# A fused attention and mixer kernel: two additions from banks and the roots of two pairs moved to VectorE, and the loads of one pair begun a step sooner

## The chip, the core and the metric

The kernel runs on one core of one Trainium2 chip. Such a core has five engines, each with its own queue of instructions, which it works in order: TensorE (PE in the profile; its weight loads are PEld) multiplies matrices, VectorE (DVE) and ScalarE (ACT) work elementwise and on rows, GpSimd (POOL) does elementwise work too, and SyncE (SP) here only issues DMA transfers. TensorE writes to banks of PSUM; everything else lies in SBUF or in DRAM. Engines wait for each other by semaphores.

The metric is the device time of one execution in microseconds, start to end. A kernel's time is the median of several executions.

## The reference

Attention with normalized queries and keys, then one mixer layer, all in fp32:

```python
# B, H, S, D = 8, 12, 448, 64;  d_model = H*D = 768, d_tok = 256, d_ch = 1536
rmsnorm = lambda x, g: x / sqrt(mean(x * x, -1) + 1e-6) * g
scores = matmul(rmsnorm(q, g_q), rmsnorm(k, g_k).T) / sqrt(D)
attn = exp(scores - max(scores)); attn = attn / (sum(attn) + 1e-9)
x = concat_heads(matmul(attn, v))                     # (B, S, 768)
h = relu(x.T @ w_tok1) @ w_tok2                       # over the sequence
u = x + h.T
out = u + relu(u @ w_ch1) @ w_ch2                     # over the channels
```

The four mixer weights arrive in 64 bits and are converted on the chip. The eight batch entries are independent of each other but for the weights.

## The kernel before

**Pairs and elements.** The 96 heads are worked as 48 pairs of heads, six to a batch entry, which the text calls an element: pairs 0 to 5 belong to element zero, 6 to 11 to the next, 12 to 17 to element two, 18 to 23 to element three. The mixer of one element runs while the attention of the next one or two is computed between its products, so that TensorE always has work.

**Queries, keys and roots.** `Start.loads` (L1280) gives the DMAs of a pair: four for a *plain* pair (below 12), which lies in rows and is turned by TensorE, and eight of 56 KB for a pair from 12 on, which is loaded in *blocks* of 32 rows (L1296) and turned by VectorE's 32 x 32 transposes. A pair's q and k lie together in one of two slots (`qk_t[p % 2]`, L1287), so the loads of pair p + 2 wait until pair p has been turned. For each pair ScalarE squares (`square`, L1312, L1315), VectorE sums over the head dimension (`reduce`, L1329), and for pairs in blocks ScalarE copies the half sums across (`fold`, L1337). The inverse roots are made for two pairs at a time: a first guess from the bits of the number (`guess`, L1351, VectorE) and three Newton steps (`newton`, L1354). A step is four GpSimd instructions (L1359 to L1362) for pairs 2 to 11 and from pair 20 on (`far`, L1221), and otherwise three on VectorE (`newton_step`, L1370 to L1372). `scale` (L348, VectorE) multiplies the pair by the roots, and `turn_qk` (L350) transposes it.

**Attention steps.** Up to pair 17 the attention goes in small steps (`att_step(g)`, L584, with g = 4t + s and s from 0 to 3 for the two pairs 2t and 2t + 1): some of the scores (L386, with ScalarE's exponentials at L390), products with the values (L459), and beside them the preparation of the next two pairs. From t = 9 (`BIG`, L513) it goes in large blocks (`big_step`, L515), whose first one, in place of step 36, squares pairs 20 and 21 and takes their roots. In the kernel before, L691 loads pair 21 in step 35, and L682 loads pair 20 in the same step, eight DMAs each; steps 34 and 35 belong to pairs 16 and 17 and also turn pairs 18 and 19.

**Weights.** `weight_items` (L313) walks over the chunks of the raw weights: load (L181), four conversion instructions on VectorE (L273 to L278), one on ScalarE (L284), a last one on VectorE (L307), and a store (L197) of the converted chunk, called a *stage*, to DRAM. From a stage's four blocks GpSimd makes four sums (`make`, L209 to L212) for the products with fewer multiplications that the later elements use. For the first eight stages the blocks are loaded again into spare tiles called `few` (L226), added there and stored (L216); these rounds lie in the second half of element zero's products (`first_items`, L1059). The later elements read blocks and sums as *units* of 384 KB (`load_units`, L841), into eight tiles.

**The mixer.** Element zero uses the stages directly: `tok1` (L764), `tok2` (L806, whose bank VectorE adds to u at L811, one addition per 128 channels), then `first_stage` (L883) for each of the 36 stages, 18 of the channel mixer's first matrix and 18 of its second. Two banks of PSUM (`ps_M`, two buffers) take turns in all of these. A column of banks is closed six stages apart for the second matrix: stages 23, 29 and 35. There ScalarE copies each of two banks to SBUF (L903) and GpSimd adds it to u (L904). Two `turns` (L1015, VectorE) then transpose the last channels for the output, which goes out by 32 rows at a time.

Element one and the later ones have x turned through DRAM: VectorE transposes (L752), `send_x` (L714) writes to `xs`, `load_x` (L723, L726) reads it back. Then `tok1`, `tok2`, and `moving_sums` (L819), which makes four sums called T1 to T4 of u's quarters, the first two on VectorE, the last two on GpSimd. The products `ch1` (L922) and `ch2` (L979) run in the order of `PRODUCTS` (L817); the fourth of them reads T3. `ch2` adds to u by VectorE and GpSimd (L988).

**What sets the order.** On TensorE, VectorE, ScalarE and GpSimd the order is the program's own. The lists of work carry a cost with each item, and `merge` (L27) and `place` (L565) mix two lists in proportion to these costs; `later` (L119) puts a DMA off by some microseconds of the same costs. A changed list thus changes the places of what it is mixed with. SyncE's queue alone is ordered by the compiler's planner, by its own estimate of when each transfer is ready to go. SyncE then works it in order: a DMA that waits holds up all behind it.

Of the kernel before, what the change touches and what calls it, by code (L numbers as in the profile page):

```python
# [13 lines left out]
ALU = mybir.AluOpType  # L14
# [30 lines left out]
def whole(ctx, tc, shifted, pre, q, k, v, g_q, g_k, moe_w_tok1, moe_w_tok2, moe_w_ch1, moe_w_ch2, out):  # L45


    nc = tc.nc
# [64 lines left out]
    st = dict(pre.st)  # L113
# [317 lines left out]
    def on_pe(p):  # L431

        return shifted or p < NPAIR
# [14 lines left out]
    def values(ps, k):  # L448

        kw = dict(start=(k == 0), stop=(k == NK - 1))  # L450
        for p in ps:
            if k == 0:
                st["o", p] = ps_O.tile([P, 512], F32, name="o_ps")
                if on_pe(p):
                    st["d", p] = s_tile("d_ps") if shifted else m_tile()
            e, vt = exps(p, k), st["v", p]
            for a in range(2):
                rows = rows_of(p, a)
                nc.tensor.matmul(  # L459
                    out=st["o", p][a * D:(a + 1) * D, 0:S], lhsT=vt[rows, k * D:(k + 1) * D], rhs=e[rows, :], **kw)  # L460
        for p in ps:
            if on_pe(p):
                ones(p, exps(p, k), **kw)
        if not shifted:
            used(ps[0] // 2, k)
# [47 lines left out]
    BIG = NPAIR + NPAIR // 2  # L513
# [70 lines left out]
    def att_step(g):  # L584


        t, s = divmod(g, 4)
        p = 2 * t
        pair = (p, p + 1)
        live = g < NG  # L590
        items = []

        def finish():
            if s == 0 and t:
                last = (p - 2, p - 1)
                for k in (NK - 2, NK - 1):
                    values(last, k)
            if live:
                for k in ((0,), (1, 2), (3, 4), (5, 6))[s]:
                    score(t, k)  # L600
            if s == 0 and t:
                if not on_pe(p - 1):
                    row_sums(t - 1)
                for i in last:
                    st.pop(("v", i))

        def tiled():
            if shifted:
                if live:
                    both_shifted()  # L610
            else:
                finish()
            if live and s == 3:
                for i in pair:
                    st.pop(("qkT", i))
            if inside:
                for fn in turns:
                    fn()
            if live and s and not shifted:
                for k in ((), (0,), (1, 2), (3, 4))[s]:  # L620
                    values(pair, k)

        def both_shifted():
            i = p + s // 2
            if s % 2 == 0:
                score_shifted(i)
                return
            for k in range(NK):
                values((i,), k)
            for k in range((NK + 1) // 2):  # L630
                st.pop(("e1", i, k))
            st.pop(("v", i))
            for part in denominators((i,)):
                part()

        n = p + 2
        ahead, behind, turns = [], [], []
        f = lambda fn, *pairs: [lambda i=i: fn(i, st) for i in pairs]  # L640
        scales = lambda n: [lambda i=i: scale(i) for i in (n, n + 1)]
        if g in (1, 5):
            ahead, behind = f(pre.square, g // 4 * 2 + 4), f(pre.reduce, g // 4 * 2 + 4)
        elif g in (2, 6):
            ahead, behind = f(pre.square, g // 4 * 2 + 5), f(pre.reduce, g // 4 * 2 + 5)
        elif g in (3, 7):
            behind = pre.roots(g // 4 * 2 + 4, st)
        elif g in (4, 8):
            behind = scales(g // 4 * 2 + 2)
        if live and n < NP:  # L650
            late = n < 2 * NPAIR + 2
            if t >= NPAIR // 2 and late:
                if s == 1:
                    ahead, behind = f(pre.square, n), f(pre.reduce, n) + f(pre.square, n + 1)
                elif s == 2:
                    behind = f(pre.reduce, n + 1) + pre.roots(n, st) + scales(n)
            elif t >= NPAIR // 2:
                a, b = f(pre.square, n) + f(pre.reduce, n), f(pre.square, n + 1) + f(pre.reduce, n + 1)
                behind = (a, b + pre.roots(n, st), scales(n), [])[s]
            now = {2: [] if pre.plain(n) else [n], 3: [n, n + 1] if pre.plain(n) else [n + 1]}.get(s, [])  # L660
            turns = [lambda q=q, i=i: turn_qk(q, i) for q in now for i in (1, 0)]

        inside = g < 2 * NPAIR
        items += [(0.3, fn) for fn in ahead]
        items.append((2.4 if s == 1 else 3.2, tiled))
        part = lambda fns, c=0.4: [(c, fn) for fn in fns]
        if s == 0 and t and not shifted:
            items += part(denominators((p - 2, p - 1)))
        soon = s == 3 and not inside and not pre.plain(n)
        if soon:  # L670
            items += part(turns)
        if live and not on_pe(p):
            items += [(0.5, lambda k=k: group_sums(t, k)) for k in ((), (1, 2), (3, 4), (5, 6))[s]]

        if s == 0 and 5 < p + 1 < NP:
            items.append((0.0, lambda: load_v(p + 1)))
        if live and s == 1 and 5 < p + 2 < NP:
            items.append((0.0, lambda: load_v(p + 2)))
        js = []
        if live and s == 0:  # L680
            js = [n, n + 1] if pre.plain(p) else [n + 1]
        elif live and s == 3 and not pre.plain(n):  # L682
            js = [n + 2]
        items += [it for j in js if pre.first_slot + 2 <= j < NP
                  for it in part(pre.loads(j, st, nc.sync, nc.sync), 0.2 if pre.plain(j) else 0.6)]
        if g == 3:
            items += [it for j in (6, 7) for it in part(pre.loads(j, st, nc.sync, nc.sync), 0.2)]
        items += part(behind)
        if not inside and not soon:
            items += part(turns)  # L690
        if g == 4 * BIG - 1 and not shifted:  # L691
            items += part(pre.loads(n + 3, st, nc.sync, nc.sync), 0.3)
        return items


# [169 lines left out]
    def r_tile(i):  # L865
        return r_pool.tile([P, 2 * HS], F32, name=f"r{i}")
# [16 lines left out]
    def first_stage(n):  # L883

        w, _, m, t = stages[n]
        wide = w is moe_w_ch2
        last = (KF if wide else KC) - 1
        if t == 0:
            st["m", 0], st["m", 1] = m_tile(), m_tile()
        a, u = st.pop(("stage", n)), st["uT", 0]  # L890
        for o in range(2):
            ps = st["m", o][:, 0:S]
            for half in range(2):
                nc.tensor.matmul(  # L894
                    out=ps, lhsT=a[:, o + 2 * half, :],
                    rhs=natural(half)[:, :, t, :] if wide else u[:, half * KC + t, :],
                    start=(t == 0 and half == 0), stop=(t == last and half == 1))
            if t < last:
                continue
            if wide:  # L900

                to, c = u[:, o * KC + m, :], r_tile(1 + o)[:]
                nc.scalar.copy(out=c, in_=ps)  # L903
                nc.gpsimd.tensor_tensor(out=to, in0=to, in1=c, op=ALU.add)  # L904
            else:
                nc.scalar.activation(
                    out=natural(o)[:, :, m, :], in_=ps.rearrange("p (i n) -> p i n", i=2), func=AF.Relu)
        st["used"].add(("stage", n))
# [178 lines left out]
    stages = stage_list()  # L1087
# [20 lines left out]
    for p in (4, 5):  # L1108
# [7 lines left out]
        out=g_t[:, 0:1], in0=g_t[:, 0:1], scalar=float(D) ** 0.5, in1=g_t[:, 1:2],  # L1116
# [27 lines left out]
    for b in range(B):  # L1144
# [33 lines left out]
        elif b + AHEAD < B:  # L1178
            t = (b + AHEAD) * NPAIR // 2
# [18 lines left out]
class Start:  # L1198
# [155 lines left out]
    def newton(self, p, st, last):  # L1354
        nc, x, y = self.nc, st["x", p], st["y", p]
        t = self.nt_pool.tile([128, 56], F32, name="nt", tag="nt")[0:y.shape[0], 0:y.shape[1]]
        if 1 < p < 2 * self.NPAIR or p >= self.far:

            nc.gpsimd.tensor_tensor(out=t, in0=y, in1=y, op=ALU.mult)  # L1359
            nc.gpsimd.tensor_tensor(out=t, in0=t, in1=x, op=ALU.mult)  # L1360
            nc.gpsimd.tensor_scalar(t, t, -0.5, 1.5, ALU.mult, ALU.add)
            nc.gpsimd.tensor_tensor(out=y, in0=t, in1=y, op=ALU.mult)  # L1362
        else:
            self.newton_step(x, y, t)
        if last:
            del st["x", p], st["y", p]
# [80 lines left out]
```

## Time and profile before

The median of three executions was 1307.17 us, from 1307.05 to 1308.61. One more was profiled:

| quantity | value |
|---|---|
| profiled execution, whole | 1308.48 us |
| its span, first to last instruction | 1306.6 us |
| granted TensorE clock | 0.99 of full |
| TensorE busy | 1260.9 us (97%) |
| VectorE busy | 763.7 us (58%) |
| ScalarE busy | 375.9 us (29%) |
| GpSimd busy | 351.3 us (27%) |
| moved by DMA | 229.59 MB, 176 GB/s in the mean |

By stretches of the span the engines' busy time and the mean busy share of the 16 DMA engines are:

| stretch, us | what runs on TensorE | TensorE busy, us | VectorE, us | GpSimd, us | DMA share |
|---|---|---|---|---|---|
| 0 to 110 | attention of element zero | 90.59 | 89.11 | 22.52 | 0.75 |
| 110 to 284 | mixer of element zero, attention of element one | 162.05 | 123.59 | 47.23 | 0.74 |
| 284 to 435 | mixer of element one, attention of element two | 146.52 | 98.17 | 70.97 | 0.92 |
| 435 to 1306.6 | all that follows | 861.74 | 452.86 | 210.60 | 0.66 |

In the lines of the timeline that follow below, a line has the start in us from the span's start, the busy us, the engine, the kernel's line, the operation, the tiles written and read with partitions x elements, and how many instructions the line stands for; the bracket has the engine's idle time before it and what ended it. SPq is SyncE's queue of issues, and the us there are the time that the issues took. In lines of waits the numbers are the sum of the idle time in us, the count, and the longest. A tile's name stands for all its buffers: `m_ps` are the two banks of `ps_M`, `stage` the converted weights. Ends of matmuls are modelled, and times on GpSimd are rough.

### The profile page before, as it was taken

The numbers are of one execution on the slowest core, as the hardware profiler recorded it, in microseconds if no ns is written. First come the engines' busy times: TensorE is split into PE (matmuls) and PEld (weight loads), VectorE is DVE, ScalarE is ACT, GpSimd is POOL, SyncE is SP. The second block draws the span as 40 slices with busy tenths as digits, with TensorE's granted clock in tenths as the row PEclk, the third lists the DMA queues.
The fourth block names the chain that finished last, engine by engine and source line by source line (L and its number), as shares of the span: only waits on it lengthen the run. The fifth ranks groups of instructions, "written<-read, shape, count | busy, mean of one in ns | idle before, by whom it ended". The sixth has DMA issues, their size and how long they took to land.

```text
span 1306.6 us, 20357 instructions
## 1 busy us (share of the span) xinstructions
PE 1260.9 (97%) x7408; PEld 927.2 (71%) x7408; DVE 763.7 (58%) x1205; ACT 375.9 (29%) x752; POOL 351.3 (27%) x575
## 2 busy tenths in 40 slices
PE   5998999989998999999999999999999999999996
PEld 3444444447787687796778777896788868797996
DVE  6998868827774466645676366754656366433212
ACT  6663423214331134302442043312342033200100
POOL 1302410447452222231332122331232123111220
PEclk9999999989998999999999999999999999999999
DMA  9666485899988776695648767685767865386554
GB/s 210 171 186 179 117 225 151 201 260 253 245 197 207 175 168 167 145 248 115 162 130 197 187 150 174 158 226 110 177 157 160 225 139 139 113 225 144 172 172 90
DMA packets 506131, 229.59 MB, mean 176 GB/s; under 512 B 375460, under 2 KB 467620, under 8 KB 506020
## 3 DMA queue, kind: packets, MB, share of 16 engines
q1 hardware_dynamic: 492898, 226.34, 69.6%
q10 hardware_dynamic: 12994, 1.84, 0.8%
q8 instruction: 61, 1.00, 0.3%
q14 instruction: 50, 0.41, 0.1%
q0 software_dynamic: 128, 0.00, 0.0%
HBM read 188.58 MB, written 39.52 MB: 175 GB/s over the span
## 4 chain that ended last, share of the span: by engine, by line
PE 83%; DVE 6%; DMA 4%; SPq 2%; issue 2%; POOL 2%; ACT 1%; DVEq 0%; ACTq 0%; POOLq 0%
PE m_ps L922 26%; PE m_ps L979 25%; PE s_ps L386 9%; PE o_ps L459 8%; PE m_ps L806 5%; PE m_ps L764 2%; PE t_ps L764 2%; PE m_ps L894 2%; DMA raw<-in_moe_w_ch_dram 1%; PE d_ps L439 1%; DVE raw L274 1%; DVE raw L276 1%; PE m_ps L439 1%; DMA hb<-in_q_dram 1%; DVE es L427 1%
## 5 line engine op out<-in xcount | busy, mean ns | idle before, releaser
L979 PE MATMUL m_ps<-hb,unit 128*128 128x224 f32 x1764 | 342.3, 355 | 4.3 <-DVE uT L988 4.3
L979 PEld LDWEIGHTS m_ps<-hb,unit 128*128 128x128 f32 x1764 | 334.5, 191 | 15.6 <-issue 10.5
L922 PE MATMUL m_ps<-tu,unit 128*128 128x224 f32 x1008 | 201.7, 355 | 0.0
L922 PEld LDWEIGHTS m_ps<-tu,unit 128*128 128x128 f32 x1008 | 189.1, 190 | 14.1 <-issue 9.2
L390 ACT ACTIVATE e<-s_ps 128x448 f32<-128x448 f32 x294 | 138.5, 552 | 207.4 <-PE s_ps L386 199.3
L922 PE MATMUL m_ps<-uT,unit 128*128 128x224 f32 x756 | 151.0, 354 | 0.0
L922 PEld LDWEIGHTS m_ps<-uT,unit 128*128 128x128 f32 x756 | 142.3, 190 | 6.7 <-issue 5.3
L386 PE MATMUL s_ps<-qkT 64*64 64x448 f32 x1260 | 143.7, 545 | 0.8 <-ACT x L747 0.8
L459 PE MATMUL o_ps<-e,v 64*64 64x448 f32 x1148 | 129.4, 538 | 0.3 <-ACT uT L496 0.2
L988 POOL TENSOR_TENSOR uT<-uT,r 128x448 f32<-128x448 f32 (+1 forms) x56 | 56.6, 1022 | 229.0 <-DVE r L988 138.5
L427 DVE TENSOR_TENSOR es<-es,e 128x896 f32<-128x896 f32 x90 | 109.1, 1212 | 13.8 <-ACT e L390 8.5
L927 DVE TENSOR_TENSOR r<-m_ps,r 128x448 f32<-128x448 f32 x63 | 39.2, 622 | 108.0 <-PE m_ps L922 55.8
L988 DVE TENSOR_TENSOR uT<-uT,m_ps 128x448 f32<-128x448 f32 (+1 forms) x70 | 33.7, 498 | 114.2 <-PE m_ps L979 114.2
L386 PEld LDWEIGHTS s_ps<-qkT 64*64 64x64 f32 x1260 | 44.9, 132 | 69.0 <-issue 58.7
L459 PEld LDWEIGHTS o_ps<-e,v 64*64 64x64 f32 x1148 | 44.9, 133 | 62.9 <-issue 58.9
L806 PE MATMUL m_ps<-w_sb,h 128*128 128x448 f32 x192 | 78.1, 560 | 10.3 <-DVE uT L811 10.3
L927 POOL TENSOR_TENSOR hb<-r,r 128x448 f32<-128x448 f32 x21 | 24.1, 1147 | 235.8 <-ACT r L943 227.2
L806 PEld LDWEIGHTS m_ps<-w_sb,h 128*128 128x128 f32 x192 | 36.6, 195 | 48.0 <-issue 27.3
L928 ACT ACTIVATE hb<-hb 128x448 f32<-128x448 f32 x63 | 36.3, 577 | 117.3 <-DVE hb L927 98.6
L1329 DVE TENSOR_REDUCE ms<-sq 128x28 f32<-128x896 f32 (+2 forms) x44 | 47.5, 1079 | 35.6 <-ACT sq L1315 32.8
L348 DVE TENSOR_TENSOR qk_t<-qk_t,rs 128x896 f32<-128x896 f32 (+1 forms) x42 | 54.2, 1327 | 15.5 <-POOL rs L1362 15.3
L811 DVE TENSOR_TENSOR uT<-uT,m_ps 128x448 f32<-128x448 f32 x48 | 29.2, 613 | 54.2 <-PE m_ps L806 54.0
(132 smaller groups left out, 1417.5 us busy)
## 6 DMA issues: line engine op xcount, KB each, us to landing
unit<-ws SPq DMA_DIRECT2D x294, 384.0 KB, 4.2
raw<-in_moe_w_ch_dram SPq DMA_DIRECT2D x72, 256.0 KB, 3.7
v<-in_v_dram SPq DMA_DIRECT2D x96, 112.0 KB, 3.8
xs<-xt SPq DMA_DIRECT2D x56, 168.0 KB, 5.0
out_dram<-turned SPq DMA_DIRECT2D x168, 56.0 KB, 1.9
qk_t<-in_q_dram SPq DMA_DIRECT2D x144, 56.0 KB, 3.2
qk_t<-in_k_dram SPq DMA_DIRECT2D x144, 56.0 KB, 3.5
x<-xs SPq DMA_DIRECT2D x42, 192.0 KB, 3.4
```

The lines of the kernel that those rows point to most:

```text
L348: nc.vector.tensor_tensor(out=x, in0=x, in1=r.unsqueeze(2).to_broadcast(list(x.shape)), op=ALU.mult)
L386: nc.tensor.matmul(out=pss[i][rows_of(i, a), 0:S], lhsT=qkT[h, 1, k * D:(k + 1) * D], rhs=qkT[h, 0, :], start=True, stop=True)
L390: nc.scalar.activation(out=e[:, i, :], in_=pss[i][:, 0:S], func=AF.Exp)
L427: nc.vector.tensor_tensor(out=es[:], in0=(es if k > 1 else st["e", t, 0])[:], in1=st["e", t, k][:], op=ALU.add)
L459: nc.tensor.matmul(out=st["o", p][a * D:(a + 1) * D, 0:S], lhsT=vt[rows, k * D:(k + 1) * D], rhs=e[rows, :], **kw)
L764: nc.tensor.matmul(out=st["t1", h][jc][:, 0:HC], lhsT=w1_sb[:, c, jc * P:(jc + 1) * P], rhs=st["x", b, h][:, :, c, :], start=start and c = ...
L806: nc.tensor.matmul(out=ps[:, 0:S], lhsT=st["h1", jc][:, cc * P:(cc + 1) * P], rhs=w2_sb[:, jc].rearrange("p c r -> p (c r)"), start=(jc == ...
L922: nc.tensor.matmul(out=ps[:, j * HS:(j + 1) * HS], lhsT=w[:, t, j, :], rhs=m, start=(t == 0), stop=(t == KC - 1))
L927: add = lambda e, o, x, y: e.tensor_tensor(out=o, in0=x, in1=y, op=ALU.add)
L979: nc.tensor.matmul(out=ps[:, j * HS:(j + 1) * HS], lhsT=st["w"](j, t), rhs=hb[:, HB[what], t, :], start=(t == 0), stop=(t == KF - 1))
L988: add = lambda e, o, x, y: e.tensor_tensor(out=o, in0=x, in1=y, op=ALU.add)
L1329: self.nc.vector.tensor_reduce(out=st["ms", p][:, p % 2, lo:hi], in_=sq[:, lo:hi], axis=AX_X, op=ALU.add)
```

## The change

Four edits:

- `first_stage`, for the last stage alone (stage 35, which closes the last channels' two banks): VectorE adds the bank to u directly, in place of ScalarE's copy and GpSimd's addition. Stages 23 and 29 are as before.
- `newton`: the bound for GpSimd falls from pair 12 to pair 8, so that the roots of pairs 8 and 9 (p = 8) and of pairs 10 and 11 (p = 10) are made by VectorE's `newton_step`. Pairs 2 to 7 and from 20 on stay with GpSimd.
- `att_step`, L682 and L691: the loads of pair 20 move from step 35 to step 34, and those of pair 21 stay in step 35. Both now follow the turns of their step, and each DMA is given a cost of 0.3 where pair 20's had 0.6.
- In the branch for large gains (`shifted`, not run with these inputs) the loads are as before.

```diff
@@ att_step
-        elif live and s == 3 and not pre.plain(n):
+        elif live and s == 3 and not pre.plain(n) and (shifted or t < BIG - 1):
             js = [n + 2]
...
-        if g == 4 * BIG - 1 and not shifted:
-            items += part(pre.loads(n + 3, st, nc.sync, nc.sync), 0.3)
+        if t == BIG - 1 and s > 1 and not shifted:
+            items += part(pre.loads(n + s, st, nc.sync, nc.sync), 0.3)
@@ first_stage
             if wide:
-
                 to, c = u[:, o * KC + m, :], r_tile(1 + o)[:]
+                if n == len(stages) - 1:
+                    nc.vector.tensor_tensor(out=to, in0=to, in1=ps, op=ALU.add)
+                    continue
                 nc.scalar.copy(out=c, in_=ps)
                 nc.gpsimd.tensor_tensor(out=to, in0=to, in1=c, op=ALU.add)
@@ Start.newton
-        if 1 < p < 2 * self.NPAIR or p >= self.far:
+        if 1 < p < self.NPAIR + 2 or p >= self.far:
```

## The prediction

> **What bounds the kernel now.** I read first the page's engine totals: TensorE is busy 97% of the span, VectorE 58%, GpSimd 27%. A gain can only come out of TensorE's 45.7 us of idle time, so the second view is TensorE's waits, by what ended them:
>
> ```profile
> PE t_ps L360 <- DVE g_t L1115: 15.0, 1, 15.0
> PE m_ps L806 <- DVE uT L811: 10.3, 3, 6.2
> PE m_ps L979 <- DVE uT L988: 4.3, 1, 4.3
> PE m_ps L894 <- ACT r L903: 2.2, 1, 2.2
> PE m_ps L894 <- DVE stage L307: 1.2, 1, 1.2
> ```
>
> The first lies at the kernel's beginning, where nothing changes. The rest sum to 18.0 us, all between 107 and 416 us, and all name VectorE or ScalarE. Which of the 10.3 us lies where, and what VectorE itself was waiting for, the timelines of the two engines tell (start, us, engine, line, operation; in brackets the idle time before it and who ended it):
>
> ```profile
> 105.82 2.30 DVE L348 TENSOR_TENSOR qk_t<-qk_t,rs 112x1024 f32<-112x1024 f32 x1 [3.91 <-POOL rs L1362]
> 108.70 1.77 PE L806 MATMUL m_ps<-w_sb,h 128*128 128x448 f32 x4 [1.60 <-DVE uT L811]
> 113.42 2.50 PE L806 MATMUL m_ps<-w_sb,h 128*128 128x448 f32 x4 [2.56 <-DVE uT L811]
> ...
> 255.94 9.29 PE L894 MATMUL m_ps<-hb,stage 128*128 128x448 f32 x24 [1.18 <-DVE stage L307]
> 281.89 0.65 DVE L1015 STREAM_TRANSPOSE turned<-uT 128x448 f32<-128x448 f32 x1 [23.45 <-POOL uT L904]
> 284.18 8.36 PE L806 MATMUL m_ps<-w_sb,h 128*128 128x448 f32 x16 [6.18 <-DVE uT L811]
> ```
>
> VectorE stood 23.45 us behind one addition of GpSimd (L904, starting at 280.7), and L811, which frees TensorE's bank, is queued behind that turn. The third place is in the SyncE timeline and ScalarE's:
>
> ```profile
> 384.55 0.97 SPq L714 DMA_DIRECT2D xs<-xt  x2
> ...
> 404.07 2.13 SPq L1296 DMA_DIRECT2D qk_t<-in_k_dram  x3
> 406.82 0.45 SPq L853 DMA_DIRECT2D unit<-ws  x1
> 407.32 0.45 SPq L1296 DMA_DIRECT2D qk_t<-in_k_dram  x1
> 411.75 0.95 ACT L1315 ACTIVATE sq<-qk_t 128x896 f32<-128x896 f32 x1 [7.94 <-DMA qk_t<-in_k_dram]
> ```
>
> The last load of pair 21 is issued at 407.32 and, by the chain of waits, takes 4.36 us; the square, the reduction and the folded copies follow, and behind them in VectorE's queue stands the addition L988 that TensorE waits 4.30 us for. After 435 us TensorE works 861.7 of 871 us, and nothing of the change lies there.
>
> **What the Trainium skill says.** "Trainium Kernel Development and Optimization", Key Constraints: GpSimd cannot access PSUM. That is why a bank went by a ScalarE copy (528 ns mean) and a GpSimd addition (1238 ns); VectorE does both in one instruction, and the trace agrees with L811, the same addition from a bank, at 613 ns. "GPSIMD Engine Reference", 3.1 Elementwise: an fp32 addition of two tensors takes GpSimd about twice VectorE's time; the small operations here agree less (254 ns against 190 undisturbed), but GpSimd needs four per step to VectorE's three. "SBUF — State Buffer", Who interferes with whom: a VectorE instruction with two SBUF inputs contends with a GpSimd one that reads SBUF. The trace agrees: L348 takes 1.15 us when GpSimd idles, 2.30 at 105.82 where GpSimd's `few` additions run, and those grow from 0.46 to 1.32.
>
> **Roots of pairs 8 and 10.** Each loses 12 GpSimd and gains 9 VectorE instructions; 112x32 ones took 190 ns at the start (L1370 to L1372), some 0.25 with the gap to the next, so 2.3 us. For pair 8, VectorE idled 3.91 us and then ran L348 disturbed. In its place: roots 101.9 to 104.2, L348 undisturbed to 105.4, first L811 to 106.0 against 108.65: TensorE, free at 107, no longer waits 1.60. L348, five conversion instructions and the next L811 follow; the additions of `few`, now free of the roots, run against them, so I take the same 2.6 us, between 1.3 and 3. TensorE stands 2.6 earlier at 113.4. For pair 10, VectorE waited until 149.9; with the roots behind the conversion that ends at 147.5 it is at 149.6: nothing by itself, and up to 1.7 us worse if `few` collides (the disturbed ones at 300 us took 0.33 to 0.46). It is hidden by the conversions' lead over TensorE there, 30 us.
>
> SyncE's order moves too. GpSimd being free, the planner puts six more `few` stores and loads between 111 and 121 us. A round is a load (3.0), four additions (1.9), a store (2.4); I walked SyncE's queue with these: pair 9's values, issued at 125.4 and landed at 129.8, now land at 130.4 to 132.8, and TensorE reads them at 131.9 less 2.6. I give back 1.1 of the 2.6 (bounds 0 and 3.5). Weight loads of 118 to 138 come 3 to 6 us later, under slack of 5 to 11; those of 160.2 and 168.7, which waited behind `few`, come 7 to 10 earlier, and so do the q and k loads at 174.0, which held SyncE, ScalarE (6.37 us at 196.5) and VectorE.
>
> VectorE then starts its dense stretch at 199.2 when its own scores allow, 1.8 earlier on top of 1.5. From there it is back to back to 257, and the conversion is just in time at 255.9 (1.18 wait). So TensorE comes to 265 earlier by 1.5 + 1.8 = 3.3; its other 2.2 wait is within that. Bounds: +1 and -6.0 (2.6 + 3.4).
>
> **Last banks.** Two copies and two GpSimd additions go, two VectorE additions of 0.61 come. VectorE has been idle since 258.4, so they run as TensorE closes the banks (263.8, 265.3), ready at about 265.9 where ScalarE gave them at 265.85. Both turns follow, and their buffers were sent at 241 and 254; L811 then answers each pair of L806 at once. The 6.18 us go. What is late next: TensorE's fourth product (308.4) reads T3, whose last third GpSimd made at 303.98, behind sums whose load is queued on SyncE at 295.2 after eight L704 throttled by unit loads. That chain moves by only 3.3, to 300.7; TensorE, 3.3 + 6.2 earlier, wants it at 298.9: 1.8 to 1.9 back. Net 4.3 (bounds 2 and 6.2).
>
> **Loads of pair 20.** Eight DMAs go from step 35 to step 34 behind the turns of pair 18; the step list's total falls from 7.2 to 4.8 of cost, which shifts two attention blocks behind one or two more products (2.3 and 4.3 us), no work added. SyncE is blocked from 377 to 384.5 anyway; the first loads go at about 382.3. Of pair 21 only two q and four k parts stay behind the x loads (397.65): 6 x 0.55 and 3.5 landing, about 404 against 411.7. The square is no longer late and the 4.3 go. Late next: unit 37, which stands behind the transfer of xs at 417.5; TensorE, without its stop, needs it at 419.1, where it lands at 419.2. Back 0 to 2; I take 0.8. Net 3.5.
>
> **Sum.** 3.3 + 4.3 + 3.5 = 11.1 us. The profiled execution has span 1306.6 and 1.9 around it, 1308.48; less 11.1 is 1297.4. It stood 1.3 above the median of 1307.17, so 1296.1.
>
> **Rivals.** First, all three gains hold and nothing is given back: 6.0 + 6.2 + 4.3 = 16.5, 1290.7; for it speaks the unit loads' lead of 7 to 20 us in most of 295 to 400, against it the T3 chain and 1.4 to 2.2 us at units 33, 34 and 38. Second, element one is bound by its transfers: the DMA engines are busy 92% from 284 to 435, and a TensorE that comes earlier waits for units; then of 11 only the 4.3 of the loads or the like remains, 1303. Against it: most unit loads there are issued when TensorE frees a buffer, so they come along. Third, the change of the loads does nothing, SyncE being blocked by xs: 7.4 to 7.6, 1299.6. Slower: the `few` rounds, put on SyncE ahead of weight and value loads at 111 to 146. Each load behind them waits for additions and a store to land. If the walk above is short by a half, the loads come not 6 but over 12 us late, more than the slack of 5 to 11; the conversion loses that, and at 255.9, with no lead, TensorE stops for it. It decides once the loss there passes the 7.8 of the other two parts: 11 lost gives 1310.5. For it speaks that SyncE is in order; against it, that the loads of 160 to 175 lose the same rounds.
>
> **Numbers.** Likeliest 0.57, by itself 1293 to 1300; all gains 0.12; transfers 0.14; loads idle 0.05; within 0.2% (2.6 us, about what a measurement tells from no change) 0.05; slower 0.07. The 8 in 10 are 1290.5 to 1303.5. Faster by over 0.2%: 0.87; within: 0.06; slower: 0.07.
>
> **What would show it.** Right: no wait before L806 near 275 us and none of 4 us before the ch2 products near 400; the VectorE wait of 23 us on GpSimd gone; VectorE's root instructions near 102 us at 0.2 to 0.3; pair 21's last load landed 6 us or more before TensorE's need; a short TensorE or GpSimd wait at T3. Wrong: a wait for values near 130 longer than 3 us; conversions no earlier at 255; waits of TensorE for units in element one; an unchanged 4 us wait behind L988.

## The result, and the profile after

The changed kernel takes 1314.78 us (median of six runs, 1311.41 to 1317.40), the kernel before beside it 1306.65 (six runs). The ratio is 1.0063, 95% interval 1.0044 to 1.0083: slower by 0.6%, where 0.8% faster was forecast and 1303.5 was the upper end of the range. The profiled execution took 1315.66 us, its span 1313.9 us.

TensorE's waits in the changed kernel (line waited for and releaser: us in total, count, longest). The kernel before's lines from 903 on have moved by two: L922 is L924 now, L979 is L981, L988 is L990.

```profile
PE o_ps L459 <- DMA v<-in_v_dram: 5.6, 1, 5.6
PE m_ps L924 <- POOL tu L829: 3.5, 2, 2.4
PE m_ps L924 <- DVE hb L929: 3.1, 1, 3.1
PE m_ps L894 <- DVE uT L811: 2.4, 1, 2.4
PE m_ps L981 <- DMA unit<-ws: 2.0, 1, 2.0
PE m_ps L894 <- DVE stage L307: 1.5, 1, 1.5
PE m_ps L806 <- DVE uT L811: 1.5, 1, 1.5
...
PE m_ps L981 <- DVE uT L990: 0.6, 1, 0.6
```

Each wait that the change aimed at is gone or shorter: of 10.3 us before L806 1.5 are left, of 4.3 before the ch2 products 0.6. Others stand in their place, and the first is one for the values of pair 9, near 131 us. TensorE's own busy time rose too, from 1260.9 to 1264.7 us for the same 7408 matmuls. The changed kernel by stretches shows why (busy us and instructions of PE, PEld, DVE, ACT, POOL; then the granted clock, the DMA share, GB/s):

```profile
124.00:137.00 13.00, 7.18 (x32) 3.00 (x33) 8.04 (x16) 2.79 (x5) 2.59 (x6) 0.96 0.93 217
137.00:143.00 6.00, 5.98 (x9) 2.40 (x10) 2.19 (x2) 0.18 (x1) 0.17 (x1) 0.51 1.15 282
143.00:150.00 7.00, 7.00 (x44) 3.03 (x42) 3.54 (x6) 4.19 (x8) 2.95 (x7) 1.00 0.42 115
```

After its stop, which ends at 137.0, TensorE works for 6 us at half its clock.

How far TensorE is ahead (-) or behind (+) of the kernel before, at the start of the same product in the two traces:

| where in the kernel before, us | product | changed kernel, us |
|---|---|---|
| 100.8 | first `tok2` of element zero | +0.4 |
| 122.6 | last `tok2` of element zero | -4.0 |
| 135.9 | fourth of the 36 stages | +8.3 |
| 236.6 | 28th stage | +4.8 |
| 274.8 | first `tok2` of element one | +5.1 |
| 290.9 | last `tok2` of element one | -3.4 |
| 310.8 | fifth `ch1` product | +3.3 |
| 330.3 | eleventh `ch1` product | +4.7 |
| 358.7 | nineteenth `ch1` product | +10.3 |
| 415.9 | first product of the second `ch2` group | +6.6 |
| 434.7 to the end | | +7.8 |

So the change wins 4.4, then 8.5, then 3.7 us where it was to win, and loses 12.4 at 123 to 136, 6.7 at 291 to 311, and 5.6 at 330 to 359. The three losses are to be explained.

### The profile page after: what moved, and what is told of

Same layout as the page of the kernel before. It is cut to its first block, busy times and chain, and to the rows that moved or that the text cites. A ratio compares the mean times of both kernels' runs of the same rounds, so it can differ in the third digit from the quotient of the medians.

```text
span 1313.9 us, 20347 instructions
## 1 busy us (share of the span) xinstructions
PE 1264.7 (96%) x7408; PEld 928.1 (71%) x7408; DVE 762.3 (58%) x1225; ACT 375.1 (29%) x750; POOL 339.0 (26%) x549
## 4 chain that ended last, share of the span: by engine, by line
PE 82%; DVE 9%; DMA 3%; SPq 2%; issue 2%; ACT 1%; POOL 1%; DVEq 0%; ACTq 0%; POOLq 0%
PE m_ps L981 25%; PE m_ps L924 24%; PE s_ps L386 8%; PE o_ps L459 8%; PE m_ps L894 5%; PE m_ps L806 5%; PE t_ps L764 2%; PE m_ps L764 2%; PE d_ps L439 1%; DVE raw L274 1%; DVE raw L276 1%; DVE es L427 1%; DVE ms L1331 1%; DMA raw<-in_moe_w_tok_dram 1%; PE m_ps L439 1%
## 5 line engine op out<-in xcount | busy, mean ns | idle before, releaser
L981 PE MATMUL m_ps<-hb,unit 128*128 128x224 f32 x1764 | 341.5, 355 | 2.6 <-DMA unit<-ws 2.0
L981 PEld LDWEIGHTS m_ps<-hb,unit 128*128 128x128 f32 x1764 | 333.5, 191 | 14.1 <-issue 11.4
L924 PE MATMUL m_ps<-tu,unit 128*128 128x224 f32 x1008 | 205.4, 358 | 3.5 <-POOL tu L829 3.5
L924 PEld LDWEIGHTS m_ps<-tu,unit 128*128 128x128 f32 x1008 | 191.7, 193 | 18.3 <-issue 9.9
L924 PE MATMUL m_ps<-uT,unit 128*128 128x224 f32 x756 | 152.8, 356 | 4.7 <-DVE hb L929 3.1
L924 PEld LDWEIGHTS m_ps<-uT,unit 128*128 128x128 f32 x756 | 143.1, 191 | 12.8 <-issue 5.3
L427 DVE TENSOR_TENSOR es<-es,e 128x896 f32<-128x896 f32 x90 | 108.8, 1209 | 15.0 <-ACT e L390 10.1
L990 POOL TENSOR_TENSOR uT<-uT,r 128x448 f32<-128x448 f32 (+1 forms) x56 | 56.2, 1014 | 233.7 <-DVE r L990 145.0
L929 DVE TENSOR_TENSOR r<-m_ps,r 128x448 f32<-128x448 f32 x63 | 39.3, 623 | 118.9 <-PE m_ps L924 67.0
L990 DVE TENSOR_TENSOR uT<-uT,m_ps 128x448 f32<-128x448 f32 (+1 forms) x70 | 33.8, 499 | 111.5 <-PE m_ps L981 111.5
L929 POOL TENSOR_TENSOR hb<-r,r 128x448 f32<-128x448 f32 x21 | 23.8, 1135 | 241.8 <-ACT r L945 235.1
L806 PE MATMUL m_ps<-w_sb,h 128*128 128x448 f32 x192 | 75.1, 544 | 1.5 <-DVE uT L811 1.5
L811 DVE TENSOR_TENSOR uT<-uT,m_ps 128x448 f32<-128x448 f32 x48 | 29.3, 613 | 58.6 <-PE m_ps L806 58.5
L806 PEld LDWEIGHTS m_ps<-w_sb,h 128*128 128x128 f32 x192 | 35.7, 190 | 37.5 <-issue 27.3
L894 PE MATMUL m_ps<-hb,stage 128*128 128x448 f32 x144 | 55.7, 543 | 1.9 <-DVE stage L307 1.5
```

Source lines behind the costliest of these rows:

```text
L427: nc.vector.tensor_tensor(out=es[:], in0=(es if k > 1 else st["e", t, 0])[:], in1=st["e", t, k][:], op=ALU.add)
L806: nc.tensor.matmul(out=ps[:, 0:S], lhsT=st["h1", jc][:, cc * P:(cc + 1) * P], rhs=w2_sb[:, jc].rearrange("p c r -> p (c r)"), start=(jc == ...
L894: nc.tensor.matmul(out=ps, lhsT=a[:, o + 2 * half, :], rhs=natural(half)[:, :, t, :] if wide else u[:, half * KC + t, :], start=(t == 0 an ...
L924: nc.tensor.matmul(out=ps[:, j * HS:(j + 1) * HS], lhsT=w[:, t, j, :], rhs=m, start=(t == 0), stop=(t == KC - 1))
L929: add = lambda e, o, x, y: e.tensor_tensor(out=o, in0=x, in1=y, op=ALU.add)
L981: nc.tensor.matmul(out=ps[:, j * HS:(j + 1) * HS], lhsT=st["w"](j, t), rhs=hb[:, HB[what], t, :], start=(t == 0), stop=(t == KF - 1))
```

## The experiments

Times are medians, ratios are to the kernel before on the same chip. The traces compare single executions, and half clock comes and goes between these: the profiled ones lie up to 3.7 us from their kernel's median (last banks alone at 1309.61, its median 1305.92; loads at 0.45 at 1300.40, its median 1303.40; the kernel before 1.3 above that of its first three runs). The loads at 0.45, which change nothing ahead of 340 us, stand 4.0 us ahead there in their trace. So a change of TensorE's shift from one product to the next, with the wait beside it, says where time goes; how much is left at the end, the ratio alone says. The recorded expectations give the rival accounts letters, theories A to G, each explained where it first stands.

### The three parts apart

**Roots of pairs 8 to 11 alone.**

```diff
-        if 1 < p < 2 * self.NPAIR or p >= self.far:
+        if 1 < p < self.NPAIR + 2 or p >= self.far:
```

> The kernel before with the roots of pairs 8 to 11 on VectorE and nothing else. Theory A (SyncE's queue): GpSimd, free of the roots, lets the rounds of few stand earlier on SyncE, pair 9's values land some 8 us later, TensorE waits 5 to 6 us for them near 131 us and then works some 6 us at about half the clock. Then 4 us won by 121 us are lost, TensorE is some 8 us behind by 145 and 5 by 265, and the time is 4 to 7 us above the kernel before. Theory B (VectorE): the 18 more root instructions hold VectorE up; the time rises too, but TensorE's waits near 131 name VectorE and not the values' DMA. Theory C (element one): the loss of the changed kernel comes from the other two edits; then this one is 2 to 4 us faster than before or the same.

1312.84 us, ratio 1.0049 (1.0035 to 1.0063), as theory A expected. TensorE is 4.5 us ahead at the last `tok2` and 8.0 behind at the fourth stage, with 4.2 us of waiting for pair 9's values between. This part makes most of the loss. Theory C falls as far as it says that all the loss comes later.

**Last banks alone.**

```diff
+                if n == len(stages) - 1:
+                    nc.vector.tensor_tensor(out=to, in0=to, in1=ps, op=ALU.add)
+                    continue
```

> The kernel before with the last two banks of stage 35 added by VectorE and nothing else. Theories A and B: TensorE comes 8 us earlier to the fourth product of element one (the 6.2 us stop and about 2 us of slow clock after it are gone), and waits there some 4 us for T3, whose chain on SyncE and GpSimd doesn't move; net 2 to 5 us faster than before. Theory C: the wait for T3 and slow clock after it take back all and more, the same as before or up to 4 us slower.

1305.92 us, ratio 0.9992 (0.9982 to 1.0002): less than theories A and B expected, and what theory C says of this kernel, the same as before. TensorE goes from 0.3 ahead at the first `tok2` of element one to 8.9 ahead at the last, and is 0.2 ahead by the eleventh `ch1` product. Its timeline shows most of the way back (start, us, engine, line; in brackets the idle time and who ended it), with the stretch that follows below it:

```profile
300.86 0.65 PE L924 MATMUL m_ps<-tu,unit 128*128 128x224 f32 x2
302.77 0.65 PE L924 MATMUL m_ps<-tu,unit 128*128 128x224 f32 x2 [1.26 <-POOL tu L829]
305.77 5.62 PE L924 MATMUL m_ps<-tu,unit 128*128 128x224 f32 x20 [2.35 <-POOL tu L829]
```

```profile
305.70:309.00 3.30, 3.23 (x9) 2.94 (x10) 0.00 (x0) 0.00 (x0) 3.22 (x9) 0.50 0.97 276
```

The fourth product wants T3. GpSimd, in order, makes it behind sums whose load it waited 10.4 us for:

```profile
300.13 0.61 POOL L209 TENSOR_TENSOR raw<-raw 128x128 f32<-128x128 f32 x1 [10.37 <-DMA raw<-ws]
...
302.05 0.66 POOL L829 TENSOR_TENSOR tu<-uT 128x224 f32<-128x224 f32 x1
...
305.06 0.66 POOL L829 TENSOR_TENSOR tu<-uT 128x224 f32<-128x224 f32 x1
```

The last 1.6 us go at 327.58, where eight products with the values take 2.57 us (0.93 in the kernel before): SyncE issued these values at 322.29, in the kernel before at 322.30, and they landed at 328.43.

**Loads of pair 20 alone.**

```diff
-        elif live and s == 3 and not pre.plain(n):
+        elif live and s == 3 and not pre.plain(n) and (shifted or t < BIG - 1):
...
-        if g == 4 * BIG - 1 and not shifted:
-            items += part(pre.loads(n + 3, st, nc.sync, nc.sync), 0.3)
+        if t == BIG - 1 and s > 1 and not shifted:
+            items += part(pre.loads(n + s, st, nc.sync, nc.sync), 0.3)
```

> The kernel before with pair 20's loads in step 34 and nothing else. Theories A and B: pair 21's last load lands some 7 us earlier, the 4.3 us wait of TensorE behind L988 near 412 goes, and a wait of 0 to 2 us for a unit comes; 2 to 4 us faster than before. Theory C: the wait for the unit takes back more, within 1.5 us of before.

1306.94 us, ratio 0.9995 (0.9986 to 1.0004), what theory C says of this kernel. Where L988 had held TensorE, at 416 us, 3.7 us are won; 1.7 had been lost at 351 us, with a wait of 1.5 for L927 that the kernel before does not have:

```profile
352.99 2.54 PE L922 MATMUL m_ps<-uT,unit 128*128 128x224 f32 x12 [1.47 <-DVE hb L927]
...
416.82 4.81 PE L979 MATMUL m_ps<-hb,unit 128*128 128x224 f32 x24 [0.59 <-DVE uT L988]
423.70 8.56 PE L979 MATMUL m_ps<-hb,unit 128*128 128x224 f32 x44 [2.08 <-DMA unit<-ws]
```

**Last banks and loads together**, without the roots.

> The changed kernel with the roots of pairs 8 to 11 back on GpSimd: last banks and loads alone. Theory A and B: no wait for values near 131 us, 5 to 9 us faster than the kernel before, 12 to 16 us faster than the changed kernel. Theory C: no faster than the kernel before.

1307.68 us, ratio 1.0007 (0.9998 to 1.0015): what theory C said of this kernel, and not the 5 to 9 us of theories A and B. Theory A is thus right for the roots and wrong on the other two edits, which do not make the kernel slower, but do not make it faster either. So two causes are wanted: one for the roots' loss, one for where two gains went.

### What costs the roots their gain

**Pairs 8 and 9 alone**, and **pairs 10 and 11 alone**:

```diff
+        if 1 < p < 2 * self.NPAIR and p != 8 or p >= self.far:    # pairs 8 and 9 by VectorE
...
+        if 1 < p < self.NPAIR + 4 or p >= self.far:               # pairs 10 and 11 by VectorE
```

> The kernel before with the roots of pairs 8 and 9 alone on VectorE; those of pairs 10 and 11 stay with GpSimd and, standing in its queue until 144 us, hold back all later rounds of few as before. If SyncE's queue and those rounds cost the changed kernel its time (theory A): TensorE is 3 to 4.5 us earlier by 121 us and keeps it past 145, no wait for values, 1 to 4 us faster than before. If the root instructions on VectorE cost it (theory B): TensorE is late by 145 as with both roots, less about half, 2 to 4 us slower.

> The kernel before with the roots of pairs 10 and 11 alone on VectorE. Theory A: two more rounds of few go on SyncE before pair 9's values, these land some 4 us or more later than before, and TensorE waits for them near 131 us, though no VectorE instruction was added before that time; 3 to 8 us slower. Theory B: TensorE as before up to 150 us, the time within 2 us of before.

The first gives 1303.06 us, ratio 0.9981 (0.9974 to 0.9989): faster. The second was run once: 1312.69 us, above all 42 runs of the kernel before beside it (1301.73 to 1308.63, median 1305.77). Its trace makes it the sharpest of the experiments. In the second kernel TensorE stops 4.9 us for the values:

```profile
131.88 0.92 PE L459 MATMUL o_ps<-e,v 64*64 64x448 f32 x4
137.71 2.34 PE L459 MATMUL o_ps<-e,v 64*64 64x448 f32 x4 [4.91 <-DMA v<-in_v_dram]
```

and VectorE's first added instruction, L1370 for pair 10, comes 19 us after that stop has ended:

```profile
153.98 0.18 DVE L1351 TENSOR_SCALAR rs<-ms 112x32 int32<-112x32 int32 x1
...
156.93 0.18 DVE L1370 SCALAR_TENSOR_TENSOR nt<-rs 112x32 f32<-112x32 f32 x1
```

So the roots on VectorE cannot be the cause of this stop, and theory B falls. What moved ahead of the stop is GpSimd's queue: with pair 10's roots in it, it stood in front of them from 114 to 145 us, and the rounds of `few` that follow in the program waited behind. SyncE's queue in the kernel before, then in the changed one, then in the kernel with pairs 10 and 11:

```profile
114.12 0.36 SPq L216 DMA_DIRECT2D ws<-few  x1
114.53 1.21 SPq L181 DMA_DIRECT2D raw<-in_moe_w_ch_dram  x2
115.79 0.60 SPq L197 DMA_DIRECT2D ws<-stages  x1
116.50 0.44 SPq L226 DMA_DIRECT2D few<-ws  x1
...
125.38 1.30 SPq L336 DMA_DIRECT2D v<-in_v_dram  x2
```

```profile
111.75 3.97 SPq L216 DMA_DIRECT2D ws<-few  x2
...
118.31 0.45 SPq L226 DMA_DIRECT2D few<-ws  x1
120.87 4.45 SPq L216 DMA_DIRECT2D ws<-few  x2
125.41 0.45 SPq L226 DMA_DIRECT2D few<-ws  x1
...
132.28 1.29 SPq L336 DMA_DIRECT2D v<-in_v_dram  x2
```

```profile
118.47 6.67 SPq L216 DMA_DIRECT2D ws<-few  x2
...
133.10 1.29 SPq L336 DMA_DIRECT2D v<-in_v_dram  x2
```

A store alone is issued in 0.36 us. In the changed kernel two pairs of stores took 3.97 and 4.45, since the second of each waits for GpSimd's additions, and those of the second pair for a load of `few` that lands 4.3 us after its issue; all behind such a store waits too: 8.4 less 4 x 0.36 is 7.0 us of standing still. SyncE stood elsewhere as well, in both kernels. From the store that it has issued at about 99 us to the values it stood still for 14.8 us in the kernel before and 21.3 in the changed one, and issued for 11.4 us in both: so the values are issued 6.9 us later. Their transfers then took some 0.9 us longer to land.

**The order kept.** To hold the rounds where they were, GpSimd gets instructions of the same size in the roots' place, whose result nobody reads; once with the roots alone on VectorE, once in the changed kernel.

```diff
+            if p in (8, 10):
+                d = self.rs_0[0:y.shape[0], 0:y.shape[1]]
+                nc.gpsimd.tensor_tensor(out=d, in0=x, in1=x, op=ALU.mult)
+                nc.gpsimd.tensor_tensor(out=d, in0=d, in1=x, op=ALU.mult)
+                nc.gpsimd.tensor_scalar(d, d, -0.5, 1.5, ALU.mult, ALU.add)
+                nc.gpsimd.tensor_tensor(out=d, in0=d, in1=x, op=ALU.mult)
```

> The kernel before with the roots of pairs 8 to 11 on VectorE, and GpSimd given as many instructions of the same size in their place, whose result nobody reads. SyncE's order of transfers is then that of the kernel before. Theory A (the order of SyncE's queue is what costs): TensorE 3 to 4.5 us earlier by 121 us as with the roots alone, no wait for values near 131, 1 to 5 us faster than before. Theory B (VectorE's 18 more instructions cost): 2 to 6 us slower, as the roots alone were.

> The changed kernel with the same idle GpSimd instructions in place of the roots it lost. Theory A: the wait for values goes and the time falls by 8 to 13 us against the changed kernel, to 1 to 5 us below the kernel before. Theory B: within 2 us of the changed kernel.

1308.93 us, ratio 1.0025 (1.0013 to 1.0038), and 1310.92 us, ratio 1.0040 (1.0026 to 1.0055). Both ratios are lower than without the idle instructions (1.0049 and 1.0063), though the intervals overlap. Theory A had expected both kernels to be faster than the kernel before, and they are not; the first time is even in the range that theory B named, and the second lies between the two. But theory B has no place for it: pair 8's roots on VectorE alone win time, and pair 10's come here at 149.9 us, behind the loss. The order on SyncE was kept (in the first of these kernels all of its 1199 transfers, in the second all up to 310 us); its times were not. GpSimd's idle instructions ran against VectorE's `scale`, and in the first of these kernels two of the twelve took 1.21 and 2.21 us in place of 0.25:

```profile
103.97 1.21 POOL L1370 TENSOR_TENSOR rs<-rs,ms 112x32 f32<-112x32 f32 x1
105.25 0.24 POOL L1367 TENSOR_TENSOR rs<-ms 112x32 f32<-112x32 f32 x1
105.57 2.21 POOL L1368 TENSOR_TENSOR rs<-rs,ms 112x32 f32<-112x32 f32 x1
```

The chain ended at 109.2 and not at 105.8, the two stores of `few` went at 111.1 and 117.95 and not at 108.5 and 114.1, and everything behind them by as much later: the raw weights, for which VectorE now idled, and behind it the addition that frees TensorE's bank,

```profile
122.75 0.43 DVE L273 TENSOR_SCALAR cv_sb<-raw 128x512 uint32<-128x512 uint32 x1 [4.01 <-DMA raw<-in_moe_w_ch_dram]
...
125.00 0.61 DVE L811 TENSOR_TENSOR uT<-uT,m_ps 128x448 f32<-128x448 f32 x1
```

and the values. That makes a series, in which the same queue is late by different amounts:

| kernel | SyncE stood still, us (before: 14.8) | values issued, against before, us | TensorE's shift at 122.6 | at 135.9 | lost between |
|---|---|---|---|---|---|
| pairs 8 and 9 | 13.7 | -2.1 | -4.2 | -3.0 | 1.2 |
| idle instructions, roots alone | 18.9 | +3.6 | -2.2 | +2.4 | 4.6 |
| idle instructions, changed kernel | 18.8 | +4.1 | -3.8 | +2.7 | 6.5 |
| roots alone | 21.2 | +6.6 | -4.5 | +8.0 | 12.5 |
| changed kernel | 21.3 | +6.9 | -4.0 | +8.3 | 12.4 |
| pairs 10 and 11 | 22.0 | +7.7 | -0.9 | +9.2 | 10.1 |

Where the queue is 4 us late some 5 us are lost, where it is 7 us late 10 to 12, with or without added VectorE instructions before the stop; pairs 10 and 11 lose less than the two rows above them, having come to the values with 3 us less of a lead. Theory A stands by this series and by the kernel with pairs 10 and 11; that the order alone, with the old times, would have kept the gain was not reached, since nothing was tried that holds the rounds back and leaves GpSimd free.

### Where the other gains went

**T3 by VectorE**, added to the last banks:

```diff
-        nc.gpsimd.tensor_tensor(out=T3, in0=B12, in1=B22, op=ALU.subtract)
+        (nc.vector if b == 1 else nc.gpsimd).tensor_tensor(out=T3, in0=B12, in1=B22, op=ALU.subtract)
```

> The kernel before with the last banks of stage 35 added by VectorE, and in element one T3 made by VectorE (three instructions of about 0.4 us) in place of GpSimd. If the gain of the last banks goes at T3, which stands behind sums and their loads (theory D): no wait of TensorE for GpSimd near 302 and 305 us and no half clock after it, TensorE still 6 to 8 us ahead of the kernel before at 311, 3 to 7 us faster than before at the end. If the units' transfers bound element one (theory E): waits for units take the place of the waits for T3, and the time is within 2 us of before.

1306.77 us, ratio 1.0004 (0.9996 to 1.0012): theory D's gain did not come, the time is theory E's. The wait for T3 is gone and TensorE keeps 9.1 us of lead past 311, 318 and 323 us, as theory D said; then it loses all of it in one place, to a transfer, but not of a unit as theory E said:

```profile
320.38 0.92 PE L459 MATMUL o_ps<-e,v 64*64 64x448 f32 x4
325.97 2.40 PE L459 MATMUL o_ps<-e,v 64*64 64x448 f32 x4 [4.67 <-DMA v<-in_v_dram]
328.30 6.92 PE L924 MATMUL m_ps<-tu,unit 128*128 128x224 f32 x22
```

These values were issued on SyncE at 320.0, in the kernel before at 322.3: 2.3 us earlier, for a TensorE that came 9.1 us earlier. In the kernel before they landed at 326.98 and were read at 329.4, so that 2.4 us were all the slack there was.

**Loads that keep the blocks' places.** The same edit as the loads alone, with 0.45 for each DMA in place of 0.3, so that the list of steps keeps its total of 7.2.

> The kernel before with pair 20's loads in step 34, each DMA at a cost of 0.45 in place of 0.3, so that the list of steps keeps its total of 7.2 and nearly all attention blocks their places. If the loads' gain of 3.7 us near 412 was lost by the blocks' shift at 346 to 351 us (theory F): no loss there, 1.5 to 3 us faster than before. If it goes into the wait for unit 37 and the clock alone (theory G): within 1 us of before, as with 0.3.

1303.40 us, ratio 0.9987 (0.9977 to 0.9996). The wait behind L927 is 0.26 in place of 1.47; 0.9 us are lost at 351 and 3.7 won at 416. The gain's interval excludes nothing gained, and is at the lower end of what theory F expected; it overlaps that of the loads at 0.3, so that the difference in time is not shown. Its place is, in the traces: all four kernels with the loads at 0.3 wait for L927 (1.47 us, and 3.12 in the three that add the last banks), the others at most 0.76. That 0.76 is in the kernel with the last banks alone, which loses 1.4 us there with the loads as before; a part of the loss is thus not the loads'.

### Versions that keep the gains

> Roots of pairs 8 and 9 alone, last banks, T3 of element one by VectorE, and the loads of pair 20 in step 34 with 0.45 for each DMA, which keeps the step list's total at 7.2. Theories A and D: the parts add up, 3 from the roots, 5 from banks and T3, 1 to 3 from the loads, 7 to 12 us faster than before. Theory E: 0 to 4 us faster.

Pairs 8 and 9, last banks, T3 and loads at 0.45: 1300.23 us, ratio 0.9959 (0.9949 to 0.9969). That is some 5.5 us, between the two expectations: the parts do not all add up.

> Roots of pairs 8 and 9 alone by VectorE, and pair 20's loads in step 34 at 0.45. If the two gains are independent: 3.5 to 6 us faster than before. If the second is lost behind the first: 2 to 3 us faster.

Pairs 8 and 9 and loads at 0.45 alone: 1300.08 us, ratio 0.9964 (0.9951 to 0.9976). The two gains add up, as the first expectation said (0.36%; 0.19% and 0.13% alone). Both versions beat both kernels, and the intervals do not tell them apart: banks and T3 bring nothing that can be measured here either.

## Why the prediction was wrong

**What bounds the kernel** was read rightly: TensorE's waits, in these places. But "A gain can only come out of TensorE's 45.7 us of idle time" misses that an idle time can cost more than its length, in busy time behind it. In the kernel before itself, after the 6.18 us before L806:

```profile
277.00:284.00 7.00, 1.00 (x3) 0.19 (x1) 1.67 (x3) 0.00 (x0) 6.65 (x13) 0.83 0.76 176
284.00:288.50 4.50, 4.32 (x6) 2.19 (x7) 2.11 (x5) 0.00 (x0) 4.27 (x10) 0.51 1.05 325
288.50:295.00 6.50, 6.50 (x36) 2.64 (x35) 3.74 (x8) 1.51 (x4) 1.29 (x3) 1.00 0.98 305
```

Half clock for 4.5 us is about 2.2 us lost. Every wait in the sums was priced at its idle time alone, new ones and old ones alike.

**Roots: -3.3 forecast, +5.0 in the trace** (from +0.4 at 100.8 to +5.4 at 265 us). Pair 8's step held: L348 came to 104.6 as forecast, undisturbed (the whole trace is 0.4 later there), and TensorE was 2.7 earlier by the next wait and 4.4 by the last `tok2`. The step that failed is "I walked SyncE's queue": a round was counted as a load of 3.0 us, four additions of 1.9 together and a store, and pair 9's values put at 130.4 to 132.8, 0.6 to 3.0 later than before. They landed at 137.65, 7.8 later. The walk is not written out, so that its slip can't be pointed at; what came out too small is the time that SyncE stands still, 6.5 us more than before, most of it at stores that wait for GpSimd's additions. The sizes were low: a round's additions took up to 3.65 us, being slowed down against VectorE (up to 1.31 us for one where 0.46 is the undisturbed time; the text had seen this, and priced it for VectorE only), and a load of `few` up to 4.3. The number of rounds was not low: five more stores and loads stand ahead of the values, not six, between 111 and 126 us.

The give-back was 1.1, bounds 0 to 3.5; it was 12.4, of which 5.6 are the wait for values, 2.4 that for L811, whose VectorE had waited 2.2 us for raw weights, and about 3 half clock; 1.4 are not accounted for.

A second fault: pairs 8 and 10 were priced as one edit on one engine. Pair 8's roots are the gain, and pair 10's, "hidden by the conversions' lead", are the loss, because in GpSimd's queue they had held back the rounds. The later regain at 199 to 237 us that the text spoke of is there (3.5 us), but only part of the loss was to be had back. Nor is it shown to be the roots': it is the wait of 2.21 us behind L903 with its half clock that is gone, and the trace of the loads at 0.45, which change nothing there, regains 2.9 at the same place.

**Last banks: -4.3 forecast, about -0.4 in the trace** (from +5.1 at the first `tok2` of element one to +4.7 at the eleventh `ch1` product), and 0.9992 alone. The stop of 6.18 us went, with its half clock 8.5. "What is late next" was named rightly, T3 behind the sums' load on SyncE. The sum was wrong: it let that chain come 3.3 us earlier with the roots, and T3's last third was ready 6.9 later, at 310.9 (1.7 later with the last banks alone, 4.4 with the roots alone); two waits of 1.11 and 2.36 us came, and half clock for some 6 us after. And it stopped at T3: with T3 out of the way the values at 326 take the same.

**Loads: -3.5 forecast, +3.1 in the trace** (+4.7 to +7.8), and 0.9995 alone. The gain of 4.3 behind L988 came, as 3.7, and the wait for unit 37, forecast as 0 to 2, was 2.0. The failed step is "shifts two attention blocks behind one or two more products (2.3 and 4.3 us), no work added", costed at nothing. With a block 2.3 us later, a k slot is turned and reloaded later; in the changed kernel ScalarE waited 5.9 us before the next square, VectorE 4.2 behind it, and TensorE 3.12 for the bank that L929 frees. That the shift costs is what the waits at L927 in the traces say, at 0.3 and at 0.45; the ratios don't show it, and that it goes by the k slot is read from the trace and was not tried.

**Rivals.** The slower one had the right mechanism, `few` rounds ahead of weight and value loads on SyncE, and a chance of 7%; its place was wrong, since it looked for the loss in the conversion at 255.9 (the wait there was 1.5 against 1.2) and not in the values at 131. The one by transfers was right for element one, but not by its units. Against it the text set that unit loads come along with TensorE. They hardly did; they had slack. In the kernel with the last banks and T3 the units for the products at 312 to 316 us were issued 0.8 to 2.8 us earlier, for a TensorE 9.1 us earlier, and landed 3.2 to 3.9 us ahead of their use, where the kernel before has 11 to 13. The first unit had 7.4 us of slack before for a lead of 10.1, and cost 0.96. The values had 2.4.

**Small slips** that change nothing: 147.5 and 2.3 make 149.8 and not 149.6; the chances of being faster add up to 0.88 and not 0.87; the undisturbed L348 takes 1.21 us in the trace and not 1.15.

**What the text asked to see** was the right list: a wait for values longer than 3 us was its first sign of being wrong.

## What to carry to other kernels

Taking work from an engine frees what was queued behind it, and if a planner orders the DMA queue, that work's transfers move ahead of others that were just in time; price the slack of each of those, and count a store that waits for another engine as time in which the whole queue stands. A stop that goes is worth its length only up to the next thing that isn't earlier; in this kernel's element one that was a transfer both times, the sums' load behind T3 and then the values. When a change to costs in an interleaved schedule moves a block by one product, follow what that block frees.

## What was not expected of the hardware

A wait of TensorE of 2 us or more was mostly followed by a time at half the granted clock, in lengths of some 3.4 us or twice that: in the kernel before 2.21 and 2.56 us by 3.4 us each, 4.30 by 5.6; in the changed kernel 2.00 and 3.12 by 3.4 each, 5.58 by 5.8. After 1.18, 1.48 and 1.60 us there was none, and none after one of 2.40. In the fourteen traces of this case together, half clock began during the wait or within 3.6 us of its end at 20 of the 28 waits of 2 to 3 us, at 4 of 6 of 3 to 4 us and at all 15 of over 4 us; of the 75 from 0.7 to 2 us, counted from 60 us on, it did only at three, which each had a longer wait 3 us behind them. The same wait of 3.12 us was followed by it in the changed kernel, and not in two others.

The Trainium skill, "TensorE: Matmul & The Clock Gate", Part 1, says that the array's clock falls to half after about 3.4 us of idling and returns after about 3.4 us of work, by windows that run freely. The lengths agree. The waits that were followed by it are shorter here than the idle window it states; where the two differ, these traces decide: in this kernel a stop of 2 to 3 us more often than not costs about 1.7 us more, half of 3.4.
